# Retention then squared-ReLU FFN on one core: the second pair's v loaded before w_in, its first outputs moved ahead of the first products, and five queue places moved in the first block

## The chip, the cores and the metric

The kernel runs on one core of a Trainium2 chip. The metric is the device time of one execution in microseconds (us). Before the change it is 204.03 us, the median of three runs (203.91 to 204.12).

A core has a matrix engine (PE; its weight loads are listed as PEld), a vector engine (DVE), a scalar engine (ACT), a general engine (POOL) and a queue engine (SP) which here only issues DMA transfers. Every engine works through its own instructions in program order and waits on semaphores for the others. PE writes to PSUM; DVE and ACT read PSUM and write SBUF. POOL issues DMA transfers too.

## The reference

```python
# q, k, v: (4, 8, 768, 64); gamma[h] = 1 - 2**(-5 - h); scale = 1/8
for t in range(S):
    state = gamma * state + outer(k[:, :, t], v[:, :, t])     # 64 x 64 for each head
    y[:, :, t] = scale * (q[:, :, t] @ state)
x = y.transpose(0, 2, 1, 3).reshape(3072, 512)
h = maximum(x @ w_in, 0)                                       # w_in: 512 x 2048
out = (h * h) @ w_out                                          # w_out: 2048 x 512
```

## The kernel before

The 768 time steps of a batch are cut into chunks of 128 steps, 24 chunks in all. Within a chunk the recurrence is a masked product: scores (k against q), a mask, then outputs (v against the masked scores) plus the state of the earlier chunks against q. The outputs of a chunk are written to a tile `xt`, which is the input of the FFN. The FFN goes over blocks of chunks, `BLOCKS = [4, 2, 2, ...]`: a first product with `w_in` (in four groups of 512 columns, `w_in_bf0` to `w_in_bf3`), ReLU on ACT (L855), a square on DVE (L826), and a second product with `w_out`. The second product of most pairs of chunks uses seven half-size products instead of eight, with sums of `w_out` blocks (`sum_w_out`, L334) and of `h` blocks (L1000 in the first block, L876 later) made on DVE.

**The start (L187 to L1266) is an order written out by hand.** The first four chunks are treated as two pairs: pair 0 (chunks 0, 1) and pair 2 (chunks 2, 3). For each pair the order is: scale q and k, turn them on PE, scores (`scores_pair`, L606, whose masks are DVE instructions, L623), cast v to bf16 (`cast_pair_v`, L581: L586 on POOL, or L584 on ACT), outputs (`outputs_pair`, L657, matmuls of L666), state (`state_pair`, L634, matmuls of L642, copied to `s_bd` at L653 on ACT or L655 on DVE), and `finish_pair` (L675), which adds the state's part (L682) and copies to `xt` (L694 or L696). `first_unit` (L1103, matmuls of L846) is the first product for one chunk and one group of `w_in`; with `(0,)` it makes only the half that needs columns 0 to 255 of the group. `w_in` comes from HBM in fp32 and is cast by `cast_w` (L343), one instruction for each of the four row blocks of 128 rows and each half of 256 columns; the letters G, V, S say on which engine (POOL L351, DVE L353, ACT L355) each row block is cast. `keep_awake` (L363) are matmuls on zeros while there is nothing else for PE.

All loads of the start go through SP's one queue, in the order of L187 to L196: q and k of pair 0, k of pair 2, v of pair 0, the first half of `w_in` group 0, v of pair 2 (through `between`), the second half, the two halves of group 1, groups 2 and 3.

**From the first block on, the order is a list of places.** `ffn_pieces` (L1118) yields once for each piece of FFN work on PE, and after piece n the program emits what `put(n, ...)` has filed under n. For the first block the pieces are: 5 to 16, the first products of groups 1 to 3; 17 to 32, the second products of `last_of_first` (L979), in which `plain(j)` handles chunks 0 and 1 and the seven-product scheme chunks 2 and 3. What is emitted under the same n keeps the order in which it was filed. The pieces that matter here are

- 24 after the first half of the product with `t4`, 25 after `plain(6)`, 26 after `plain(7)` and its two output copies (L1066), 27 after the second halves of two products and `u = pb + a` (L1071, on DVE by L1000), 28 and 29 after the halves of a product into `pa`, 30 after the first half of `product(pb, s3, t3)`, which writes to the PSUM that `u` reads and takes `s3` from `third_sums`.

`attend(m, scaled, places)` (L1280) files a chunk's work: `scale_kv`, `transpose_k` (PE L419, then two ACT copies to `k_bd`, L426), `scores` (L445, mask L452 on DVE), `state` and `outputs` (L513, L521; ACT copy L529). `attend2` (L1292) does the same for chunks from 8 on, in another form: `cast_k2` (L708) on POOL, a transposing DMA on SP, `scores2` and so on. `pack_constants` (L280) makes a table of decay factors for those later chunks on POOL, DVE and ACT, and `load_w_out` (L184) issues the four loads of `w_out` from POOL's queue at places 6, 8, 11 and 14.

Of the kernel before, what the change touches and what calls it, by code (L numbers as in the profile page):

```python
# [31 lines left out]
def kernel(  # L32
# [47 lines left out]
    ps_y = ctx.enter_context(tc.tile_pool(name="ps_y", bufs=1, space=bass.MemoryType.PSUM))  # L80
# [5 lines left out]
    raw_q, raw_k, raw_v = {}, {}, {}  # L86
# [22 lines left out]
    def load_pair(m, name, src, to, heads=slice(0, H)):  # L109
        b, i = chunks[m]  # L110
        if m not in to:
            t = ldpool.tile([P, 2 * H * D], FP32, name=name)
            to[m] = t.rearrange("s (h r d) -> s r h d", h=H, r=2)
        src = src[b, heads, i * C : (i + 2) * C, :].rearrange("h (s r) d -> s h r d", r=2)
        nc.sync.dma_start(to[m].rearrange("s r h d -> s h r d")[:, heads], src)
# [57 lines left out]
    def load_w_in(g, parts=1, between=None):  # L173
        t = stage_tile(NCB * FQ).rearrange("s (c f) -> s c f", c=NCB)
        n = FQ // parts
        for j in range(parts):
            if j and between:
                between()
            nc.sync.dma_start(
                t[:, :, j * n : (j + 1) * n], w_in_v[:, :, g * FQ + j * n : g * FQ + (j + 1) * n]  # L180
            )
        staged["in", g] = t
# [7 lines left out]
    load_pair(0, "kn", k, raw_k, heads_of[1])  # L190
    load_pair(2, "kn", k, raw_k)
    load_pair(0, "vn", v, raw_v)
    load_w_in(0, parts=2, between=lambda: load_pair(2, "vn", v, raw_v))
    load_w_in(1, parts=2)
    for g in range(2, NQ):
        load_w_in(g)  # L196
# [146 lines left out]
    def cast_w(kind, g, halves=(0, 1), on="VVSG"):  # L343

        src = staged[kind, g]
        dst = (w_in_bf if kind == "in" else w_out_bf)[g]
        for half in halves:
            c = slice(half * 256, (half + 1) * 256)
            for j, engine in enumerate(on):
                if engine == "G":  # L350
                    nc.gpsimd.tensor_copy(dst[:, j, c], src[:, j, c])  # L351
                elif engine == "V":
                    nc.vector.tensor_copy(dst[:, j, c], src[:, j, c])  # L353
                else:
                    nc.scalar.activation(dst[:, j, c], src[:, j, c], AF.Copy)  # L355
# [225 lines left out]
    def cast_pair_v(m, r, on_scalar=False):  # L581
        at[m]["v"] = pair_view(v_bd2s[m // 2])
        if on_scalar:
            nc.scalar.activation(at[m]["v"][:, r], raw_v[m][:, r], AF.Copy)  # L584
        else:
            nc.gpsimd.tensor_copy(at[m]["v"][:, r], raw_v[m][:, r])  # L586
# [19 lines left out]
    def scores_pair(m, group, pools, pt):  # L606
        a = at[m]
        sts = [pool.tile([P, 2, 2, C], FP32, name=name) for pool, name in pools]
        pt = pt.rearrange("s (hh r p t) -> s hh r p t", hh=2, r=2, p=2)
        a["pt", group] = pt  # L610
        for r in range(2):
            for p in range(2):
                for hh, head in enumerate(halves):
                    for j, rows in enumerate(halves):
                        nc.tensor.matmul(
                            sts[hh][rows, r, p, :],
                            lhsT=a["kT"][head, r, 2 * group + p, j * (C // 2) : (j + 1) * (C // 2)],
                            rhs=tokens_of(m, group, p, j)[head],
                            start=True,
                            stop=True,  # L620
                        )
        def mask(hh):
            nc.vector.tensor_tensor(  # L623
                out=pt[:, hh],
                in0=sts[hh][:],
                in1=maskp.rearrange("s r q t -> s r (q t)")[:, :, None, :].to_broadcast(
                    [P, 2, 2, C]
                ),
                op=ALU.mult,
            )  # L630

        return mask
# [485 lines left out]
    def ffn_pieces(tb):  # L1118
        nch = BLOCKS[tb]
        TB = nch * C  # L1120
        if tb == 0:
            first_sums, last_sums, second_products = last_of_first()
            put(11, first_sums, 0)
            put(17, first_sums, 1)
            put(26, last_sums[0])
            put(27, last_sums[1])
            for f in range(FPQ, NFB):
                hp = ps_f.tile([P, TB], FP32, name="psf")
                first_product(tb, hp[:], f, slice(0, TB))
                relu(h_of(tb, f)[:, 0], hp)  # L1130
                yield
            yield from second_products()
            return
        elif tb <= 2:

            for c in range(nch):
                for g in range(NQ):
                    first_unit(tb, g, c)
                    if c * NQ + g in (1, 2, 3) and kept:
                        next(kept[0])  # L1140
                    if c * NQ + g == 4:
                        kept.clear()
                    if tb in SEVEN and (c, g) == (1, 3):
                        first_sums, rest = seven_products(tb)
                        first_sums(slice(0, 4))
                    yield
            if tb in SEVEN:
                yield from rest()
                return
        else:  # L1150
            h_tiles(tb)
            per = 512 // TB
            if tb in SEVEN:
                first_sums, rest = seven_products(tb)
            for f0 in range(0, NFB, per):
                hp = ps_f.tile([P, per, TB], FP32, name="psf")
                for f in range(f0, f0 + per):
                    first_product(tb, hp[:, f - f0, :], f, slice(0, TB))
                relu(h_of(tb, f0, f0 + per), hp, tb in SEVEN and f0 // per in (1, 3))
                if f0 // per in (1, 2, 3) and kept:  # L1160
                    next(kept[0])
                if f0 // per == 4:
                    kept.clear()
                if f0 // per == 5 and tb in SEVEN:
                    first_sums(slice(0, 4))
                yield
            if tb in SEVEN:
                yield from rest()
                return


        def second(op, j, g, cols=slice(0, DM)):
            for fq in range(FPQ):
                f = g * FPQ + fq
                nc.tensor.matmul(  # L1175
                    op[:],
                    lhsT=h_of(tb, f)[:, 0, j * C : (j + 1) * C],
                    rhs=w_out_bf[g][:, fq, cols],
                    start=(f == 0),
                    stop=(f == NFB - 1),  # L1180
                )

        def store(op, j, cols=slice(0, DM)):
            osb = opool.tile([P, DM], FP32, name="osb")
            nc.scalar.activation(osb[:, cols], op[:], AF.Copy)
            r0 = (first[tb] + j) * C
            nc.sync.dma_start(out[r0 : r0 + C, cols], osb[:, cols])


        for j in range(nch):  # L1190
            op = ps_f.tile([P, DM], FP32, name="psf")
            for g in range(NQ):
                second(op, j, g)
                if g == NQ - 1:
                    store(op, j)
                yield


    tp, st, f = (ps_tp, "tp"), (ps_st, "st"), (ps_f, "psf")
# [30 lines left out]
    transpose_pair_k(2, 1, *f)  # L1230
    cast_pair_v(0, 0)
    cast_pair_v(0, 1)
    mask_a = scores_pair(2, 0, (st, f), spare[:, 0:1024])
    keep_awake(2)
    end_awake()
# [4 lines left out]
    outputs_pair(0, 1)  # L1240
    mask_b = scores_pair(2, 1, (tp, f), spare[:, 1024:2048])
    mask_b(0)
    mask_b(1)
    finish_pair(0, 0)
    finish_pair(0, 1)
    state_pair(0, 1, "SV")
    cast_w("in", 0, (0,), "GGGG")
    cast_pair_v(2, 0)
    cast_pair_v(2, 1, on_scalar=True)
    first_unit(0, 0, 0, (0,))  # L1250
    first_unit(0, 0, 1, (0,))
    cast_w("in", 0, (1,), "GGVV")
    outputs_pair(2, 0, ((ps_y, "y"), st))
    outputs_pair(2, 1)
    finish_pair(2, 0)
    state_pair(2, 0, "VV")
# [15 lines left out]
    parts = {}  # L1272

    def put(place, what, *args):
        parts.setdefault(place, []).append((what, args))
# [38 lines left out]
    put(20, sum_w_out, 0)  # L1314
    put(22, sum_w_out, 1, (0, 1), slice(0, 2))
    put(24, sum_w_out, 1, (0, 1), slice(2, 4))
    put(26, sum_w_out, 1, (2, 3))
    attend(4, 12, (17, 19, 21, 23, 28))
    attend(5, None, (25, 28, 30, 32, 34))
    attend(6, 30, (33, 35, 37, 39, 42))  # L1320
    attend(7, None, (38, 42, 44, 46, 49))
    packed = pack_constants()
    put(27, next, packed)
    put(34, next, packed)
    for j, t in enumerate([s_bds[2]] + ks_bd2s + v_bd2s):
        for hh in range(2):
            put(35 + 2 * j + hh, zero_off_diagonal, t, hh)
# [1 line left out]
    for j, t in enumerate(k_big):  # L1329
# [5 lines left out]
    done = [57, 62] + [70 + 8 * j for j in range(14)]  # L1335

    ahead = {
        8: (37, 41, 44, 46, 48), 9: (0, 0, 49, 51, 53), 10: (50, 54, 55, 57, 60), 11: (0, 0, 60, 63, 68)
    }
    for m, d in zip(range(PACK_FROM, NCHUNK), done):  # L1340
        attend2(m, d, done[m - PACK_FROM - 1] if m > PACK_FROM else 0,
# [58 lines left out]
```

## Time and profile before

| | |
|---|---|
| median of three runs | 204.03 us (203.91 to 204.12) |
| profiled execution, its own time | 203.7 us |
| span of its instructions | 201.9 us |
| PE busy | 196.4 us (97%), 2403 matmuls |
| DVE busy | 148.5 us (74%) |
| ACT busy | 127.8 us (63%) |
| POOL busy | 81.1 us (40%) |
| granted PE clock | 1.0 over the whole span |

The profile is one execution. The page lists busy times, the chain of work that ended last, and groups of instructions by source line; the trace can be asked for a timeline of each engine in a stretch of time. In a timeline row the first number is the start in us from the span's start, the second the busy time, then the engine, the line, the operation, output<-input, the shapes, the number of instructions merged in the row, and in brackets the idle time before it with what ended it. Rows of 16 or 32 matmuls are one stream: the time from one matmul's start to the next is what counts, since they overlap. Some matmul records are missing from the trace (2403 of 2409).

### The profile page before, as it was taken

The numbers are of one execution on the slowest core, as the hardware profiler recorded it, in microseconds if no ns is written. First come the engines' busy times: TensorE is split into PE (matmuls) and PEld (weight loads), VectorE is DVE, ScalarE is ACT, GpSimd is POOL, SyncE is SP. The second block draws the span as 40 slices with busy tenths as digits, with TensorE's granted clock in tenths as the row PEclk, the third lists the DMA queues.
The fourth block names the chain that finished last, engine by engine and source line by source line (L and its number), as shares of the span: only waits on it lengthen the run. The fifth ranks groups of instructions, "written<-read, shape, count | busy, mean of one in ns | idle before, by whom it ended". The sixth has DMA issues, their size and how long they took to land.

```text
span 201.9 us, 5925 instructions
## 1 busy us (share of the span) xinstructions
PE 196.4 (97%) x2403; PEld 167.2 (83%) x2408; DVE 148.5 (74%) x315; ACT 127.8 (63%) x259; POOL 81.1 (40%) x152
## 2 busy tenths in 40 slices
PE   8999999999999999999999999999999999999993
PEld 8688445669965998999999999999899999999883
DVE  3987899789684678777787777777787687485374
ACT  8775875164852766783785785783775766863730
POOL 8675721099930973362622084224382022200000
PEclk9999999999999999999999999999999999999999
DMA  5999999999799999889999789999999572200202
GB/s 171 356 371 398 337 200 196 252 246 291 201 229 234 103 137 160 153 202 201 211 183 221 134 145 167 230 178 204 178 148 167 157 107 54 109 0 3 104 3 106
DMA packets 92252, 36.57 MB, mean 181 GB/s; under 512 B 68544, under 2 KB 88256, under 8 KB 92224
## 3 DMA queue, kind: packets, MB, share of 16 engines
q1 hardware_dynamic: 77312, 32.52, 68.7%
q0 software_dynamic: 14912, 3.67, 20.6%
q8 instruction: 19, 0.31, 0.6%
q14 instruction: 9, 0.07, 0.1%
HBM read 27.26 MB, written 6.29 MB: 166 GB/s over the span
## 4 chain that ended last, share of the span: by engine, by line
PE 94%; DVE 2%; ACT 1%; issue 1%; DVEq 0%
PE psf L846 42%; PE psf L880 18%; PE tp L880 7%; PE psf L1175 3%; PE psf L1039 3%; PE y L363 3%; PE psf L1004 3%; PE st L747 2%; PE y L803 2%; PE y L796 2%; PE c_ps L774 2%; PE c_ps L642 1%; PE st L445 1%; PE y L521 1%; DVE osb L876 1%
## 5 line engine op out<-in xcount | busy, mean ns | idle before, releaser
L846 PE MATMUL psf<-xt,w_in_bf 128*128 128x256 bf16 (+2 forms) x879 | 92.3, 259 | 0.1
L846 PEld LDWEIGHTS <-w_in_bf 128*128 128x128 bf16 x880 | 71.2, 98 | 11.2
L855 ACT ACTIVATE h<-psf 128x512 bf16<-128x512 f32 x96 | 56.2, 595 | 21.2 <-PE psf L846 18.9
L725 POOL COPY v_bd<-v 64x512 bf16<-64x512 bf16 x32 | 21.5, 673 | 73.7 <-DVE v L717 64.8
L826 DVE TENSOR_TENSOR h<-h 128x512 bf16<-128x512 bf16 x80 | 33.6, 433 | 21.1 <-ACT h L855 20.5
L880 PEld LDWEIGHTS <-h 128*128 128x128 bf16 x288 | 26.5, 98 | 3.0 <-DVE h L826 0.3
L160 POOL DMA_DIRECT2D k_big<-in_k_dram x32 | 21.0, 674 | 0.0
L880 PE MATMUL psf<-w_sum,h 128*128 128x256 bf16 x136 | 19.1, 273 | 0.0
L880 PE MATMUL tp<-w_out_bf,h 128*128 128x256 bf16 x136 | 19.1, 273 | 0.0
L880 PE MATMUL psf<-w_sum,k_bd 128*128 128x256 bf16 x144 | 17.9, 273 | 0.0
L876 DVE TENSOR_TENSOR u<-psf,u 128x256 f32<-128x256 f32 x18 | 7.6, 424 | 11.3 <-PE psf L880 10.9
L880 PEld LDWEIGHTS <-k_bd 128*128 128x128 bf16 x144 | 13.8, 98 | 1.5
L783 ACT ACTIVATE s_bd<-c_ps 64x256 bf16<-64x256 f32 x29 | 10.7, 370 | 6.5 <-PE c_ps L774 6.5
L876 DVE TENSOR_TENSOR osb<-psf,u 128x256 f32<-128x256 f32 x26 | 10.3, 422 | 6.1 <-PE psf L880 5.8
L376 DVE TENSOR_TENSOR qs<-qn,qf 128x512 bf16<-128x512 f32 x20 | 14.0, 704 | 0.4 <-DMA qn<-in_q_dram 0.4
L784 ACT ACTIVATE s_bd<-c_ps 64x256 bf16<-64x256 f32 x29 | 11.0, 379 | 0.4
L754 DVE TENSOR_TENSOR pt<-st,cmask 128x512 bf16<-128x512 f32 x16 | 11.0, 688 | 0.1
L717 DVE TENSOR_TENSOR v<-stage,kf 128x512 bf16<-128x512 f32 x16 | 11.0, 684 | 0.0
L916 ACT ACTIVATE osb<-tp 128x256 f32<-128x256 f32 x8 | 3.1, 385 | 12.2 <-PE tp L880 12.2
L810 ACT ACTIVATE xt<-y 128x512 bf16<-128x512 f32 x16 | 9.6, 598 | 1.8 <-PE y L803 1.2
L824 ACT ACTIVATE h<-h 128x512 bf16<-128x512 bf16 x16 | 10.1, 630 | 0.5
L876 DVE TENSOR_TENSOR k_bd<-h 128x512 bf16<-128x512 bf16 x18 | 10.1, 559 | 0.3
(151 smaller groups left out, 304.7 us busy)
## 6 DMA issues: line engine op xcount, KB each, us to landing
qn<-in_q_dram SPq DMA_DIRECT2D x12, 512.0 KB, 5.5
out_dram<-osb SPq DMA_DIRECT2D x23, 256.0 KB, 2.8
stage<-in_v_dram SPq DMA_DIRECT2D x32, 96.0 KB, 4.5
stage<-in_moe_w_in_dram SPq DMA_DIRECT2D x4, 512.0 KB, 7.6
stage<-in_moe_w_in_dram SPq DMA_DIRECT2D x2, 1024.0 KB, 8.1
w_out_bf<-in_moe_w_out_dram POOLq DMA_DIRECT2D x4, 512.0 KB, 10.2
kn<-in_k_dram SPq DMA_DIRECT2D x6, 256.0 KB, 6.0
k_big<-in_k_dram POOLq DMA_DIRECT2D x32, 48.0 KB, 4.3
```

Source lines behind the costliest of these rows:

```text
L160: nc.gpsimd.dma_start(t[rows, :, p, hh, :], k[b, 2 * p + hh, (i + 3 * n) * C : (i + 3 * n + 3) * C].rearrange("(w s) d -> s w d", s=64),)
L376: engine.tensor_tensor(out=out, in0=by, in1=table[:, :, None].to_broadcast([P, H, D]), op=ALU.mult)
L717: nc.vector.tensor_tensor(out=v2.rearrange("s (u p) d -> s u p d", u=2), in0=vn, in1=kf2[:, i, :, :, None].to_broadcast([P, 2, NPAIR, D]), ...
L725: nc.gpsimd.tensor_copy(v_bd[rows, :, hh, :], v2[rows])
L754: nc.vector.tensor_tensor(out=pt[:], in0=st[:], in1=cmask2.rearrange("s r t -> s (r t)")[:, None, :].to_broadcast([P, 2 * NPAIR, C // 2]), ...
L783: nc.scalar.activation(s_bd[halves[0], :, 0, :], c[halves[0]], AF.Copy)
L784: nc.scalar.activation(s_bd[halves[1], :, 1, :], c[halves[1]], AF.Copy)
L826: nc.vector.tensor_mul(hv, hv, hv)
L846: nc.tensor.matmul(hp, lhsT=w_in_bf[g][:, cb, fq * 128 : (fq + 1) * 128], rhs=xts[tb][:, cb, cols], start=(cb == 0), stop=(cb == NCB - 1),)
L855: nc.scalar.activation(hv, hp[:], AF.Relu)
L876: nc.vector.tensor_tensor(out=out, in0=in0, in1=in1, op=op)
L880: nc.tensor.matmul(to, lhsT=left[:, j], rhs=right(j) if callable(right) else right[:, j], start=(start and j == 0), stop=(stop and j == NF ...
```

## The change

The loads: v of pair 2 is now issued directly after v of pair 0, ahead of both halves of `w_in` group 0. The start: v of pair 2 is cast right after v of pair 0, both halves on POOL (one was on ACT); the first half of `w_in` group 0 is cast by POOL, POOL, POOL, DVE (it was POOL four times), filed between the two masks of the last scores; `outputs_pair(2, 0)` stands ahead of the two half first products instead of behind them. The places: the outputs of chunk 4 go from 28 to 24; `transpose_k` of chunk 5 from 28 to 27; `sum_w_out(1, (2, 3))` is split over 26 and 27; the third sums go from 26 to 27 and the fourth from 27 to 28; `pack_constants` goes from 27 and 34 to 12 and 15; `cast_k2` of chunk 9 goes from 49 to 47.

```diff
@@ -190,7 +190,8 @@
     load_pair(0, "vn", v, raw_v)
-    load_w_in(0, parts=2, between=lambda: load_pair(2, "vn", v, raw_v))
+    load_pair(2, "vn", v, raw_v)
+    load_w_in(0, parts=2)
     load_w_in(1, parts=2)
@@ -1122,8 +1123,8 @@
             put(11, first_sums, 0)
             put(17, first_sums, 1)
-            put(26, last_sums[0])
-            put(27, last_sums[1])
+            put(27, last_sums[0])
+            put(28, last_sums[1])
@@ -1230,6 +1231,8 @@
     cast_pair_v(0, 0)
     cast_pair_v(0, 1)
+    cast_pair_v(2, 0)
+    cast_pair_v(2, 1)
     mask_a = scores_pair(2, 0, (st, f), spare[:, 0:1024])
@@ -1240,17 +1243,15 @@
     outputs_pair(0, 1)
     mask_b = scores_pair(2, 1, (tp, f), spare[:, 1024:2048])
     mask_b(0)
+    cast_w("in", 0, (0,), "GGGV")
     mask_b(1)
     finish_pair(0, 0)
     finish_pair(0, 1)
     state_pair(0, 1, "SV")
-    cast_w("in", 0, (0,), "GGGG")
-    cast_pair_v(2, 0)
-    cast_pair_v(2, 1, on_scalar=True)
+    outputs_pair(2, 0, ((ps_y, "y"), st))
     first_unit(0, 0, 0, (0,))
     first_unit(0, 0, 1, (0,))
     cast_w("in", 0, (1,), "GGVV")
-    outputs_pair(2, 0, ((ps_y, "y"), st))
     outputs_pair(2, 1)
     finish_pair(2, 0)
     state_pair(2, 0, "VV")
@@ -1314,14 +1315,15 @@
-    put(26, sum_w_out, 1, (2, 3))
-    attend(4, 12, (17, 19, 21, 23, 28))
-    attend(5, None, (25, 28, 30, 32, 34))
+    put(26, sum_w_out, 1, (2,))
+    put(27, sum_w_out, 1, (3,))
+    attend(4, 12, (17, 19, 21, 23, 24))
+    attend(5, None, (25, 27, 30, 32, 34))
     attend(6, 30, (33, 35, 37, 39, 42))
     attend(7, None, (38, 42, 44, 46, 49))
     packed = pack_constants()
-    put(27, next, packed)
-    put(34, next, packed)
+    put(12, next, packed)
+    put(15, next, packed)
@@ -1335,7 +1337,7 @@
     ahead = {
-        8: (37, 41, 44, 46, 48), 9: (0, 0, 49, 51, 53), 10: (50, 54, 55, 57, 60), 11: (0, 0, 60, 63, 68)
+        8: (37, 41, 44, 46, 48), 9: (0, 0, 47, 51, 53), 10: (50, 54, 55, 57, 60), 11: (0, 0, 60, 63, 68)
     }
```

## The prediction

> **What bounds the kernel now.** I read the chain of waits first, then the timelines of PE, DVE, ACT and POOL up to 60 us, then the waits of PE. The chain is PE's nearly from end to end, so what the change is worth is what it does to gaps on PE.
>
> ```profile
> PE 94%; DVE 2%; ACT 1%; issue 1%; DVEq 0%
> ```
>
> The same engine's timeline, at the start and in the middle of the first block:
>
> ```profile
> 14.26 1.07 PE L846 MATMUL psf<-xt,w_in_bf 128*128 128x128 bf16 x16
> ...
> 15.30 0.24 PE L666 MATMUL y<-h,v_bd 64*64 64x128 bf16 x1
> ...
> 16.24 0.62 PE L642 MATMUL c_ps<-v_bd,ks_bdp 64*128 64x128 bf16 x8
> 16.79 1.14 PE L846 MATMUL psf<-xt,w_in_bf 128*128 128x128 bf16 x16
> ...
> 44.34 0.60 PE L1004 MATMUL psf<-w_sum,h 128*128 128x256 bf16 x4 [0.21 <-DVE u L1000]
> ...
> 45.25 0.34 PE L445 MATMUL st<-qT,k_bd 128*128 128x128 bf16 x3 [0.26 <-ACT k_bd L426]
> ```
>
> In a row of n matmuls with 128 columns the starts lie 0.056 us apart ((1.07 - 0.23)/15), with 256 columns 0.109 ((0.60 - 0.27)/3). Where the matmul's tile shape changes, the next start comes 0.15 after the last one: 0.09 lost. Counting so from start to start, PE's real waits between 13 and 60 us are small: 0.05 before 15.30 (v's cast), 0.07 after 16.79 (a cast of w_in), 0.37 at 44.34, 0.42 at 45.25, 0.07 at 46.37, 0.19 at 58.89 (chunk 6's mask). Nothing else is to be had. What the start waits for is read on POOL:
>
> ```profile
> 10.56 1.16 POOL L586 CAST v_bd<-vn 128x512 bf16<-128x512 f32 x2
> 11.89 1.43 POOL L351 CAST w_in_bf<-stage 128x256 bf16<-128x256 f32 x4 [0.17 <-DMA stage<-in_moe_w_in_dram]
> 14.64 0.61 POOL L586 CAST v_bd<-vn 128x512 bf16<-128x512 f32 x1 [1.31 <-DMA vn<-in_v_dram]
> 15.93 0.92 POOL L351 CAST w_in_bf<-stage 128x256 bf16<-128x256 f32 x2 [0.69 <-DMA stage<-in_moe_w_in_dram]
> ...
> 55.31 1.44 POOL L708 CAST ks_bdp<-stage 64x512 bf16<-64x512 f32 x2
> ```
>
> By SP's issues and their times to landing, v of pair 0 landed at 10.50, the first half of w_in at 11.84, v of pair 2 at 14.58, the second half at 15.88. Each is 512 KB; the first, second and fourth follow the one before in 1.3 to 1.5, but v of pair 2 took 2.74. The trace has sixteen completion marks for each load: fifteen of v's came by 13.39, the last at 14.58. What stands beside it is one 16 KB instruction packet, started at 11.92 and busy for 0.95:
>
> ```profile
> q8 instruction: 1, 0.02, 4.0%
> ```
>
> That queue brings nineteen such packets, one for each 120 to 380 (mostly some 270) of PE's instructions; this one comes at PE's 309th, at the state of pair 0 (11.90). One of the sixteen shares is held up behind it, and every later load of the start has its sixteenth mark about 1.2 late as well.
>
> **The start.** PE's program is the same up to 12.9, so the packet comes at 11.92 again, and the same loads lie ahead of that point in the queue, in another order: v of pair 2 lands at about 12.0 (10.50 + 1.5), or 12.97 if its last share is caught; the first half of w_in then takes the place of v at 14.58. The bounds are 13.4 (its fifteen unharmed shares) and 14.6; I take 14.58, since the bytes up to there are the same.
>
> POOL casts v of pair 2 by 13.2 to 14.2. PE has finished pair 0's second state at 14.11 (last start) and does `outputs_pair(2, 0)` from 14.26 (16 matmuls, 0.23). Then the first products wait for casts. POOL's casts of w_in start 0.05 after landing and 0.34 apart ((1.43 - 0.40)/3), so the three end at 15.03, 15.38 and 15.72; the third releases PE's third matmul at 15.76, and 13 more starts (0.72) bring the last one to 16.48. `outputs_pair(2, 1)` 16.63, `finish_pair(2, 0)` 16.99, the state 17.31 where it was 16.24: 1.07 late. The first products after it (16.79 before) lost 0.07 to a cast that will then be done. Net **+1.0**, with bounds of 0.05 (w_in at 13.4: casts done at 14.5, and one more change of tile shape, 0.09, against 0.05 of wait saved) and 1.1. Even on time the second half of w_in, cast by 16.86, holds PE where it was: nothing is gained at the start.
>
> On DVE the one cast of w_in now waits for 14.58 with the second mask, the s_bd copy of L655, two casts and two more copies behind it. The mask (0.68) ends at 15.6 and the copy at 16.0; PE wants them at 16.63 and 16.99: hidden behind POOL's casts. Without that cover (w_in at 13.4) the mask is on time anyway. ACT loses one cast (0.63) and POOL gains 0.61 in a wait of 1.31; neither is on the path. On SP nothing but the order of two issues changes.
>
> **pack_constants** moves 2.1 us of POOL work (40.95 to 43.22) between w_out's third and fourth load, issued at 24.97 and 25.70. The four land 7.0 to 13.5 after issue, 3.4 apart behind one another, so the fourth is queued, not late: 0. If it did land 2.1 later, at 41.3, DVE's sums at 40.10 (41.1 with the start's delay) would lose 0.2. Its 0.7 on DVE and 0.24 on ACT go to place 15; DVE has 0.66 idle before 36.76.
>
> **The middle, times as before.** DVE now stands so:
>
> ```profile
> 41.80 0.68 DVE L341 TENSOR_TENSOR w_sum<-w_out_bf 128x1024 bf16<-128x1024 bf16 x1
> 42.40 0.72 DVE L341 TENSOR_TENSOR w_sum<-w_out_bf,w_sum 128x1024 bf16<-128x1024 bf16 x1
> 43.04 0.79 DVE L1000 TENSOR_TENSOR h<-h 128x512 bf16<-128x512 bf16 x2
> 43.86 0.42 DVE L1000 TENSOR_TENSOR u<-psf,u 128x256 f32<-128x256 f32 x1
> ```
>
> After the change chunk 4's outputs (12 matmuls, 0.67) come at 39.38, and `pb`'s last matmul starts at 42.75; `u` can start at 43.07 instead of 43.86. Behind it are the second w_sum (0.6) and the third sums, which `product(pb, s3, t3)` needs as much as `u`: 43.07 + 0.34 + 0.60 + 0.41 = 44.42, so PE is released at 44.46, where it was 44.34. The wait stays; the third sums are late now. Chunk 5's k is turned at 42.86, ACT is free of its two output copies at 43.55, and the two k_bd copies end at 44.7 before the scores at 44.90: that 0.42 goes. Chunk 5's second scores wait for the first's mask, behind the fourth sums on DVE: 46.12 against 45.99. First product of the next block at 46.34 instead of 46.59: **-0.25**. Bounds: -0.87 (all three waits gone) and +0.1 (the third sums cost as much as the k copies give).
>
> **Chunk 9's cast.** POOL made it at 67.27; it now follows chunk 8's at 56.7, for another 1.44. Under chunk 8's cast a DVE square took 0.83 and a scaling 1.10, where 0.41 and 0.68 are usual:
>
> ```profile
> 55.45 0.83 DVE L826 TENSOR_TENSOR h<-h 128x512 bf16<-128x512 bf16 x1
> 56.20 1.10 DVE L376 TENSOR_TENSOR ks<-kn,kf 128x512 bf16<-128x512 f32 x1
> 57.22 0.68 DVE L376 TENSOR_TENSOR qs<-qn,qf 128x512 bf16<-128x512 f32 x1
> ```
>
> So the scaling at 57.22 stretches by 0.42 (the square behind it starts after the cast), chunk 6's mask at 58.16 slips by as much, and PE already waits for it at 58.89. **+0.4**, bounds -0.19 (no stretch, and the wait goes) and +0.8 (both stretched). Nothing behind it waits now for chunk 9's k, whose DMA transpose has slack, so no gain.
>
> **Sum.** 203.7 + 1.0 - 0.25 + 0.4 = 204.85 for the profiled execution (span 201.9 and 1.8 around it); the median lies 0.33 above that execution: **205.2**.
>
> The Trainium skill's page "Runtime: NRT & Kernel Launch", section "Instruction fetch mechanics", says that crossing a 16 KiB block of instructions costs "one DMA tail-bump, mostly hidden". By it the load beside the packet would not be late, w_in would land at 13.4 and the sum would be 204.2. The trace agrees for PE itself, which runs on, but not for the load.
>
> **The rivals.**
> - *On time* (14%): the packet's delay falls on a share that has slack, w_in lands near 13.4. For it: fifteen of sixteen marks. Against: every load after 11.92 had a late mark. 204.03 + 0.05 - 0.25 + 0.4 = 204.2, within noise.
> - *DVE's queue drains, faster* (13%): with `u` ahead of a w_sum and the third sums, and the decay table off its queue, DVE is no longer late for PE anywhere between 41 and 59, and the waits at 44.34, 45.25, 46.37 and 58.89 (0.87 + 0.19) all go. With w_in on time: 204.03 + 0.05 - 1.06 = 203.0. It decides as long as the start costs less than 1.06; at the forecast's start it just cancels it, 204.0. For it: `u` waits behind 1.4 of sums now. Against: the third sums are wanted at the same point of PE as `u`, and now stand behind it.
> - *POOL's double cast* (8%): both DVE instructions are stretched, with the forecast's start. 204.03 + 1.0 - 0.25 + 0.8 = 205.6.
>
> **How the numbers follow.** The forecast has 65%. Its own range runs from 204.6 (the middle or the cast at its better bound) to 206.0 (all three at their worse ones). The whole range goes down to 203.7 to take in the on-time case with some of the middle; it leaves out the faster case and a little above 205.9. This measurement tells about 0.2% (0.4 us) from no change. Faster: 0.13, and 0.01 of the on-time case. Same: the other 0.13 of that, and 0.02 of the forecast. Slower: the remaining 0.63 and 0.08.
>
> **What would show it.** Right: POOL's w_in casts start near 14.6 with the wait on the w_in load, PE's first L846 has gaps of 0.3 there and the L846 row of 16.79 stands near 17.8; the L1004 row after `u` still waits, on third sums; L445 does not wait for k_bd; two POOL casts in a row near 56, and a longer wait of L521 on chunk 6's mask. Wrong: w_in's casts at 13.4, or no instruction packet near 11.9; then the sum drops by 1.0.

## The result, and the profile after

The changed kernel takes 205.59 us (median of six runs, 205.03 to 205.62), the kernel before beside it 204.06 us (six runs, 203.91 to 204.57): a ratio of 1.0067, 95% interval 1.0052 to 1.0082. It is slower by 1.5 us. The profiled execution took 205.59 us itself, and its span grew from 201.9 to 203.8 us. Lines from L194 on are numbered one higher in it, at the very end two.

The span can be cut at three points of PE that both traces have: the start of the first product with 512 columns (the start is over), the first product of the second block, and the first product of the third block. The table gives the first of them and the two stretches between them, in us, for all kernels that are spoken of below; from the third point to the last matmul it is 133.24 in each of them but one (133.73 in "the same, packet late"). Two of the 28 executions of the four kernels whose `w_in` lands late ("after", "new start alone", "after, chunk 9's cast back", "after, all casts on POOL") ran some 3 us longer at a mean granted clock of 0.98: one of 207.68 us, which is the traced one of "after, chunk 9's cast back" (hence its 24.81), and one of 208.52 us, which widens the interval of "after, all casts on POOL".

| kernel | median, us (runs) | ratio to before, 95% | start ends | first block | second block |
|---|---|---|---|---|---|
| before | 204.03 | | 20.53 | 26.07 | 18.71 |
| after | 205.59 (6) | 1.0067 (1.0052 to 1.0082) | 21.89 | 25.86 | 19.45 |
| after, old start | 204.23 (11) | 1.0011 (1.0003 to 1.002) | 20.67 | 25.86 | 19.35 |
| new start alone | 204.86 (6) | 1.0041 (1.0027 to 1.0054) | 21.74 | 26.07 | 18.62 |
| after, chunk 9's cast back | 204.77 (12) | 1.0037 (1.0029 to 1.0046) | 24.81 | 25.86 | 18.62 |
| after, packet late | 204.67 (9) | 1.004 (1.0024 to 1.0056) | 20.80 | 25.86 | 19.35 |
| after, all casts on POOL | 205.73 (4) | 1.0133 (1.006 to 1.0205) | 21.98 | 25.87 | 19.44 |
| middle alone | 203.96 (12) | 1.0008 (0.9996 to 1.0021) | 20.56 | 25.87 | 18.94 |
| middle, third sums first | 203.14 (12) | 0.997 (0.9958 to 0.9983) | 20.68 | 25.51 | 18.62 |
| the same, packet late | 203.88 (12) | 0.999 (0.9975 to 1.0005) | 20.96 | 25.51 | 18.62 |
| the same, new start, packet late | 203.45 (12) | 0.9989 (0.9976 to 1.0002) | 20.80 | 25.51 | 18.62 |

So the change cost 1.36 at the start, gave back 0.21 in the first block, and cost 0.74 in the second: 1.89, the whole growth of the span.

**The start.** The chain of waits, by engine, as the page of the changed kernel has it:

```profile
PE 84%; DVE 5%; DMA 4%; SPq 3%; issue 1%; ACT 1%; POOL 1%; DVEq 0%
```

PE had 94% of it before. The same chain of the changed kernel in order of time (start, length, what) shows what took PE's place at the start:

```profile
7.50 7.22 DMA stage<-in_moe_w_in_dram
14.77 1.23 POOL w_in_bf L352 x3
16.04 0.96 PE psf L847 x14
```

The first half of `w_in` was issued at 7.50 and landed 7.2 later; three casts of it and then PE follow one another without slack. POOL's timeline of the changed kernel:

```profile
12.09 1.18 POOL L587 CAST v_bd<-vn 128x512 bf16<-128x512 f32 x2 [0.35 <-DMA vn<-in_v_dram]
14.77 2.09 POOL L352 CAST w_in_bf<-stage 128x256 bf16<-128x256 f32 x5 [1.50 <-DMA stage<-in_moe_w_in_dram]
...
54.20 2.19 POOL L374 MEMSET v_bd<- 64x512 bf16 x4
56.45 3.40 POOL L709 CAST ks_bdp<-stage 64x512 bf16<-64x512 f32 x4
```

The v of pair 2 is early now (cast from 12.09, before from 14.64), and POOL idles 1.50 for `w_in` instead of 1.31 for v. The completion marks of the load say why: fifteen of its sixteen shares landed between 13.10 and 13.41, the last at 14.71. The 16 KB instruction packet started at 11.59 and took 0.93. In the timeline of PE the delay goes straight through:

```profile
15.35 1.65 PE L847 MATMUL psf<-xt,w_in_bf 128*128 128x128 bf16 x16 [0.66 <-POOL w_in_bf L352]
...
17.60 0.62 PE L643 MATMUL c_ps<-v_bd,ks_bdp 64*128 64x128 bf16 x8
18.15 1.07 PE L847 MATMUL psf<-xt,w_in_bf 128*128 128x128 bf16 x16
...
44.45 1.04 PE L1005 MATMUL psf<-w_out_bf,h 128*128 128x256 bf16 x8
45.92 0.61 PE L1005 MATMUL psf<-w_sum,h 128*128 128x256 bf16 x4 [0.43 <-DVE h L1001]
46.36 0.39 PE L446 MATMUL st<-qT,k_bd 128*128 128x128 bf16 x4
...
59.63 0.39 PE L522 MATMUL y<-pt,v_bd 128*128 128x128 bf16 x4
60.78 0.38 PE L522 MATMUL y<-pt,v_bd 128*128 128x128 bf16 x4 [0.76 <-DVE pt L453]
```

Sixteen matmuls with 128 columns take 1.65 (1.07 before) and begin 1.09 later; the state stands at 17.60 instead of 16.24, and the next products at 18.15 instead of 16.79.

**The first and second block.** In the same rows, PE no longer waits for `k_bd` at 46.36. It does wait at 45.92, and the releaser is `h` of L1001, the third sums, no longer `u`. At 60.78 it waits for chunk 6's mask: from start to start 0.92 are lost there. In the kernel before, the same eight matmuls lost 0.19 and stand in one row of PE's timeline:

```profile
58.48 0.79 PE L521 MATMUL y<-pt,v_bd 128*128 128x128 bf16 x8
```

DVE's timeline of the changed kernel has both causes:

```profile
44.50 0.42 DVE L1001 TENSOR_TENSOR u<-psf,u 128x256 f32<-128x256 f32 x1 [0.95 <-ACT osb L1067]
44.84 0.68 DVE L342 TENSOR_TENSOR w_sum<-w_out_bf,w_sum 128x1024 bf16<-128x1024 bf16 x1
45.44 0.75 DVE L1001 TENSOR_TENSOR h<-h 128x512 bf16<-128x512 bf16 x2
...
56.50 0.83 DVE L827 TENSOR_TENSOR h<-h 128x512 bf16<-128x512 bf16 x1
57.26 1.10 DVE L377 TENSOR_TENSOR ks<-kn,kf 128x512 bf16<-128x512 f32 x1
58.28 1.09 DVE L377 TENSOR_TENSOR qs<-qn,qf 128x512 bf16<-128x512 f32 x1
59.30 0.83 DVE L827 TENSOR_TENSOR h<-h 128x512 bf16<-128x512 bf16 x1
60.05 0.68 DVE L453 TENSOR_TENSOR pt<-st,cmask 128x512 bf16<-128x512 f32 x1
```

`u` is done in time, then one sum of `w_out` blocks and then the sums that PE needs next. Later, four operations in a row run beside POOL's four casts (56.45 to 59.85), and all four are stretched, not two.

### The profile page after: what moved, and what is told of

It reads as the page before. It is cut to its first block, busy times and chain, and to the rows that moved or that the text cites. A ratio compares the mean times of both kernels' runs of the same rounds, so it can differ in the third digit from the quotient of the medians.

```text
span 203.8 us, 5932 instructions
## 1 busy us (share of the span) xinstructions
PE 196.3 (96%) x2408; PEld 166.6 (82%) x2408; DVE 148.1 (73%) x316; ACT 127.4 (63%) x258; POOL 81.6 (40%) x152
## 4 chain that ended last, share of the span: by engine, by line
PE 84%; DVE 5%; DMA 4%; SPq 3%; issue 1%; ACT 1%; POOL 1%; DVEq 0%
PE psf L847 39%; PE psf L881 18%; PE tp L881 7%; DMA stage<-in_moe_w_in_dram 4%; PE psf L1040 3%; SPq L115 3%; PE psf L1005 3%; PE psf L1176 3%; PE st L748 2%; PE y L804 2%; PE y L797 2%; PE c_ps L775 2%; DVE h L827 1%; PE y L522 1%; PE st L446 1%
## 5 line engine op out<-in xcount | busy, mean ns | idle before, releaser
L827 DVE TENSOR_TENSOR h<-h 128x512 bf16<-128x512 bf16 x80 | 34.1, 440 | 22.6 <-ACT h L856 22.3
```

What stands on the lines that cost most here:

```text
L827: nc.vector.tensor_mul(hv, hv, hv)
```

## The experiments

**The start taken back.** The changed kernel with the loads and the hand-written start of the kernel before.

```diff
-    load_pair(2, "vn", v, raw_v)
-    load_w_in(0, parts=2)
+    load_w_in(0, parts=2, between=lambda: load_pair(2, "vn", v, raw_v))
...
-    cast_pair_v(2, 0)
-    cast_pair_v(2, 1)
...
-    cast_w("in", 0, (0,), "GGGV")
...
-    outputs_pair(2, 0, ((ps_y, "y"), st))
+    cast_w("in", 0, (0,), "GGGG")
+    cast_pair_v(2, 0)
+    cast_pair_v(2, 1, on_scalar=True)
     first_unit(0, 0, 0, (0,))
     first_unit(0, 0, 1, (0,))
     cast_w("in", 0, (1,), "GGVV")
+    outputs_pair(2, 0, ((ps_y, "y"), st))
```

> The changed kernel with the loads and the hand-written start of the kernel before; the moved places stay. If the start costs 1.36 us (the first block's 512-column products begin at 21.89 instead of 20.53 in the trace), the time falls from 205.6 to about 204.2 to 204.6, the first products are back at 14.26 and chunk 6's mask still holds PE for some 0.9. Rival, that the places cost most of it: it stays above 205.2.

Measured: 204.23 us, 1.36 less than the whole change. `w_in` landed at 11.85 again and v of pair 2 at 14.77 with its last share. The start is the larger part of the loss, and the moved places together cost 0.2 to 0.3 us in the median. Chunk 6's mask held PE for 0.50 (at 59.47) and not for the 0.9 expected; the other part of the long second block is a wait of 0.31 for a scaling at 47.97, which the experiment with the moved places alone explains.

**The new start alone.** The reverse: the kernel before with only the new loads and start.

> The kernel before with the loads and the hand-written start of the changed one, all places as before. If the start costs 1.36, 205.4; the middle then shows the old waits of 0.37 and 0.42 and chunk 6's mask the old 0.19, unless a later start gives slack there. Rival, that the start's delay is absorbed later: 204.1.

Measured: 204.86 us, some 0.5 less than expected. The start cost 1.21 in this trace (`w_in` landed at 14.57), 0.15 less than in the changed kernel. In the second block the wait for chunk 6's mask fell from 0.19 to 0.09 (18.62 instead of 18.71), while the waits of the first block stayed. The other 0.3 lies in the starting value: the profiled execution of the kernel before is 0.33 below its median, that of this kernel on its median. The timeline of PE in this kernel:

```profile
45.85 0.23 PE L446 MATMUL st<-qT,k_bd 128*128 128x128 bf16 x1
46.47 0.34 PE L446 MATMUL st<-qT,k_bd 128*128 128x128 bf16 x3 [0.39 <-ACT k_bd L427]
...
59.69 0.70 PE L522 MATMUL y<-pt,v_bd 128*128 128x128 bf16 x8
```

The `k_bd` wait that the moved places take away is here; the eight matmuls of L522 run in one row.

**Chunk 9's cast back at 49.** The changed kernel with one number changed.

```diff
-        8: (37, 41, 44, 46, 48), 9: (0, 0, 47, 51, 53), ...
+        8: (37, 41, 44, 46, 48), 9: (0, 0, 49, 51, 53), ...
```

> The changed kernel with chunk 9's cast at its old place alone. If POOL's two casts in a row cost PE the 0.74 by which the wait on chunk 6's mask grew, 204.85, with DVE's 1.09 scaling and 0.83 square behind the ks scaling back at 0.68 and 0.41 and the wait near 0.19. Rival, that the mask is late because DVE starts that stretch late: 205.6.

Measured: 204.77 us, 0.82 less than the whole change; the second block is 0.83 shorter. Its trace is of the execution of 207.68 us, which lost 2.9 us before 24 us, as the last section shows. From there on its rows can be read. DVE's timeline in this kernel, some 2.9 us later than in the changed kernel:

```profile
59.43 0.83 DVE L827 TENSOR_TENSOR h<-h 128x512 bf16<-128x512 bf16 x1
60.19 1.09 DVE L377 TENSOR_TENSOR ks<-kn,kf 128x512 bf16<-128x512 f32 x1
61.20 0.68 DVE L377 TENSOR_TENSOR qs<-qn,qf 128x512 bf16<-128x512 f32 x1
61.81 0.41 DVE L827 TENSOR_TENSOR h<-h 128x512 bf16<-128x512 bf16 x1
62.14 0.68 DVE L453 TENSOR_TENSOR pt<-st,cmask 128x512 bf16<-128x512 f32 x1
```

Without the second pair of casts the second scaling takes 0.68 instead of 1.09 and the square behind it 0.41 instead of 0.83: 0.41 and 0.42, together the 0.83 that PE waited longer in the changed kernel. The wait for the mask that is left is 0.09, where some 0.19 was expected.

**The instruction packet moved.** The changed kernel with the zero matmuls of `keep_awake` four times as wide and a quarter as many, so that PE has 108 instructions fewer ahead of the same work and fetches its next 16 KB later.

```diff
-    nc.vector.memset(still, 0.0)
+    wide = spare[:, 4096 - 4 * P : 4096]
+    nc.vector.memset(wide, 0.0)
...
-        for _ in range(4 * n):
-            nc.tensor.matmul(idle_ps[0][:], lhsT=still, rhs=still, start=True, stop=True)
+        for _ in range(n):
+            nc.tensor.matmul(idle_ps[0][:], lhsT=still, rhs=wide, start=True, stop=True)
```

> The changed kernel with every four 128-column warm-up matmuls on zeros replaced by one of 512 columns: the same PE time, 108 fewer PE instructions ahead of the first products, nothing else. If the load of w_in is late because of the instruction packet at PE's 309th instruction, the packet now comes about 13.1 to 13.4, the load lands near 13.4 to 13.9 and the time falls by about 1.0 to 1.3, to 204.3 to 204.6. Rival, that the load is late because of its place behind two v loads of 512-byte rows: it lands at 14.7 again and the time stays at 205.6.

Measured: 204.67 us, 0.1 above the range expected. The packet came at 14.55, later than the 13.1 to 13.4 expected, and the sixteen shares of `w_in` between 13.06 and 13.38, with no straggler. Place in the queue, bytes and neighbours were the same, so it is the packet that delayed the last share. The delay moved along with it: of the first half of `w_in` group 1 fifteen shares landed by 16.10 and the last at 17.38. POOL's timeline in this kernel:

```profile
12.04 1.17 POOL L588 CAST v_bd<-vn 128x512 bf16<-128x512 f32 x2 [0.32 <-DMA vn<-in_v_dram]
13.43 1.15 POOL L353 CAST w_in_bf<-stage 128x256 bf16<-128x256 f32 x3 [0.22 <-DMA stage<-in_moe_w_in_dram]
```

The timeline of PE: the first products run without a gap.

```profile
14.59 1.07 PE L848 MATMUL psf<-xt,w_in_bf 128*128 128x128 bf16 x16
```

The start ends at 20.80, 1.09 sooner than in the changed kernel, and 0.27 later than in the kernel before. Of that 0.25 is a gap between two matmuls of the state (16.50 to 16.80) in which the trace shows no wait.

**All four casts of `w_in`'s first half on POOL.** The changed kernel with `"GGGG"` where it has `"GGGV"`.

> The changed kernel with the one cast of w_in's first half that DVE makes given back to POOL. In the trace of the changed kernel POOL's first cast there took 0.52 and began together with DVE's; the others took 0.40. If DVE's cast holds POOL's up, the first cast is 0.40 again and PE's first product starts 0.1 sooner after the landing, but the fourth row block comes 0.34 after the third, so the first block's 512-column products start within 0.1 of 21.89 and the time is 205.5 to 205.7. Rival, that POOL's first cast after a wait is slow in any case: 0.52 again, and the time 0.2 higher.

Measured: 205.73 us in the median, where 205.5 to 205.7 was expected. POOL's timeline in this kernel:

```profile
14.70 2.23 POOL L352 CAST w_in_bf<-stage 128x256 bf16<-128x256 f32 x6 [1.50 <-DMA stage<-in_moe_w_in_dram]
```

Without DVE's cast beside it, POOL's first cast takes 0.40 and releases PE at 15.15; in the changed kernel it takes 0.52 and PE comes at 15.35. POOL's fourth cast then costs more than that: PE's fourth matmul waits until 16.18, and the start ends at 21.98, 0.09 later.

**The moved places alone, chunk 9's cast at its old place.** The kernel before with the places 12 to 28 of the change.

> The kernel before with the moved places of the first block alone: old loads, old hand-written start, chunk 9's cast at its old place. In the traces so far the stretch from the first 512-column product to the next block's first product is 25.86 us with the moved places and 26.07 without, whatever the start; so 0.2 below the kernel before, 203.75. Rival, that the places pay only with a late start: 204.0.

Measured: 203.96 us, no gain: the number is the rival's. The first block is 0.20 shorter, as expected, and the second 0.23 longer. DVE's timeline of this kernel:

```profile
46.07 1.73 DVE L376 TENSOR_TENSOR qs<-qn,qf 128x512 bf16<-128x512 f32 x2
```

Two scalings of 0.68 take 1.28 together in the kernel before (46.24). Here the second runs from 46.67 to 47.80, 1.13 long, and PE waits 0.31 for it at 47.85, inside this row:

```profile
47.32 0.93 PE L406 MATMUL tp<-ident,qs 128*128 128x128 bf16 x8
```

Beside it is POOL's timeline:

```profile
46.64 0.61 POOL L392 CAST v_bd<-vn 128x512 bf16<-128x512 f32 x1
```

In the kernel before, this cast of v came at 48.94, since `pack_constants` stood ahead of it on POOL:

```profile
48.94 0.61 POOL L392 CAST v_bd<-vn 128x512 bf16<-128x512 f32 x1
```

With that moved to places 12 and 15 the cast falls on DVE's scaling. In the changed kernel it misses it by 0.05: the cast ends at 47.35 and the scalings start at 47.40, because the start is a microsecond late. Where the moved places stand behind an early start ("after, old start" and "after, packet late"), the second scaling begins 0.02 after the cast and takes 1.13 again.

**The third sums ahead of the last sum of `w_out` blocks.** The kernel just shown, with the sums that PE does not need yet filed later.

```diff
-            put(28, last_sums[1])
+            put(31, last_sums[1])
...
-    put(27, sum_w_out, 1, (3,))
+    put(28, sum_w_out, 1, (3,))
```

> The same, with the third sums directly behind u on DVE, the second half of the last w_sum behind them (place 28) and the fourth sums at place 31. If the third sums, queued behind that w_sum, are what PE's 0.59 wait after u is for, the wait falls to at most 0.1 and the stretch of 25.86 to 25.3 to 25.5: 203.2 to 203.5. Rival, that the wait only moves to the next thing DVE makes (the mask of chunk 5's first scores, or q of chunk 6): 203.75.

Measured: 203.14 us, ratio 0.997 (0.9958 to 0.9983): faster than both kernels. DVE's timeline of this kernel:

```profile
43.30 0.43 DVE L1000 TENSOR_TENSOR u<-psf,u 128x256 f32<-128x256 f32 x1 [0.66 <-ACT osb L1066]
43.64 0.75 DVE L1000 TENSOR_TENSOR h<-h 128x512 bf16<-128x512 bf16 x2
44.31 0.69 DVE L341 TENSOR_TENSOR w_sum<-w_out_bf,w_sum 128x1024 bf16<-128x1024 bf16 x1
```

And PE's:

```profile
43.25 1.04 PE L1004 MATMUL psf<-w_out_bf,h 128*128 128x256 bf16 x8
44.13 0.60 PE L1004 MATMUL psf<-w_sum,h 128*128 128x256 bf16 x4
44.56 0.63 PE L445 MATMUL st<-qT,k_bd 128*128 128x128 bf16 x4
```

The wait after `u` (0.59 in the changed kernel) is gone. Of it 0.23 comes back at once as a wait for `k_bd` inside the row at 44.56, which the other wait had covered; the first block ends 0.36 sooner. DVE's second scaling now starts at 46.44, ahead of POOL's cast at 46.77, and keeps its 0.68.

**The packet late, in that kernel.** The same with the wide zero matmuls, still with the old start.

> The previous kernel with the 512-column warm-up matmuls, which put the packet 108 instructions later. If the packet is also what made v of pair 2 late in the old order, v lands at 13.4 and the second half of w_in at 14.7, and the waits of 0.05 on v's cast and 0.07 on w_in's cast go: 0.1 less than the previous one at best, the same within noise at worst. Rival, that the old order made v late: it still lands at 14.6.

Measured: 203.88 us, in the median 0.74 above the previous kernel, where 0 to 0.1 less was expected; the two intervals overlap a little. v of pair 2 did land at 13.40 instead of some 14.6 to 14.8: in the old order it was this load that the packet delayed. But the time did not follow: there is again a gap without a wait in the state's matmuls (0.45, 16.46 to 16.97), and in the profiled execution PE lost 0.49 up to 69.93 to a wait for a transpose on SP's queue. The gap in PE's timeline:

```profile
16.23 0.45 PE L643 MATMUL c_ps<-v_bd,ks_bdp 64*128 64x128 bf16 x5
16.97 0.32 PE L643 MATMUL c_ps<-v_bd,ks_bdp 64*128 64x128 bf16 x3 [0.29 <-issue]
```

**Everything at its best place.** The same again with the change's loads and start.

> The same with the changed kernel's loads and start. With w_in on time the new start has one more change of tile shape (0.09) and no wait on v's cast, so 0 to 0.1 above the previous kernel. Rival, that the new start is worth something once w_in is on time: 0.2 or more below it.

Measured: 203.45 us, ratio 0.9989 (0.9976 to 1.0002). `w_in` landed at 13.42 and the start ended at 20.80 (a gap of 0.22 again at 16.5), against 20.68 with the old start and the packet where it was. The median is 0.43 below that of the previous kernel, which is the rival's number, but the ratios to the kernel before are 0.9989 and 0.999, with nearly the same interval. In the traces the two kernels differ by the 0.49 of the transpose and by their gaps; without the gaps (0.22 and 0.45) the new start ends 0.07 later than the old one. So with its load on time no worth of the new start is shown, and no loss that can be measured.

## Why the prediction was right, and where its sizes were off

- **Direction and cause of the start.** Right. `w_in` took the place of v beside the packet, its last share was late by 1.3, and nothing was gained from the earlier v. Moving the packet alone took away 1.09 of the 1.36, and 0.25 of what was left is the gap in the state. The rival "on time" describes the kernel with the packet late, not this one. The rule quoted from the Trainium skill's page "Runtime: NRT & Kernel Launch", section "Instruction fetch mechanics", that crossing a 16 KiB block is "mostly hidden", held for PE in the changed kernel, which shows no gap beside the packet, and not for the load: 1.09 of the start went with the packet. (The packets of the kernel before follow one another after 119 to 320 of PE's recorded instructions, where the prediction has 120 to 380; nothing rests on this.)
- **Size of the start.** The term "+1.0" was 1.36. The landing was 14.71 and not 14.58 (0.13; the other kernels with this order and the early packet have 14.57 to 14.75). "Three casts 0.34 apart" held for two of three: the first took 0.52, because DVE's cast of the fourth row block ran beside it, so the third ended at 15.98 instead of 15.72. The state came at 17.60, 0.29 later than worked out. The saving of 0.07 on a later cast was there, and as much was lost at 19.00 on DVE's copy of `s_bd`. The bound of 1.1 was too low: it had the landing at 14.6 at the latest, held DVE's cast for hidden because it was off the path, and left out what it does to POOL.
- **The middle.** "-0.25" was -0.21, by the mechanism that was named: `u` early, the third sums late (0.59 at 45.92 where some 0.5 was worked out) and the `k_bd` wait gone. For the mask of chunk 5's first scores a wait of 0.13 was worked out; it was 0.07, as before. The rival "DVE's queue drains" fell on this point; with the two sums exchanged, 0.65 of its 1.06 came true (0.56 in the first block, 0.09 in the second).
- **pack_constants.** "0" was right for `w_out`: its fourth load was issued at 27.82 instead of 25.70 and landed at 39.37 instead of 39.19. What the step did not see was POOL's own queue: a cast of v moves forward by 2.3 us. In the changed kernel it costs nothing by 0.05 us; in the kernel with the moved places alone it cost the 0.31 that ate the gain.
- **Chunk 9's cast.** "+0.4" was +0.74, near the upper bound. Here the forecast's mechanism failed and that of the rival "POOL's double cast" held: both DVE instructions were stretched. The casts were taken to end just before the square. But beside DVE's work POOL's casts slow down too (0.61, 0.70, 0.95 and 0.98): the four took 3.40, where twice 1.44 was counted, and so reached the square at 59.30.
- **The sum.** The spans differ by 1.89, where 1.15 was worked out. The median moved by only 1.53, because the profiled execution of the kernel before (203.7) lay 0.3 below its median, that of the changed kernel on its median. The prediction added 0.33 for this on both sides; so the total came out only 0.4 short. That it missed by 0.4 and not by the 0.74 of the spans is luck. So is the exact number of the rival "POOL's double cast", 205.6: it had the cast right and the start at 1.0.

What stays open is the gap of 0.22 to 0.45 without a wait in the three kernels with wide zero matmuls. The traces point to PE waiting for its instructions, though no run tests it: in all three the gap stands behind PE's 448th recorded instruction and ends 2.21 to 2.28 after the packet started (14.55, 14.68 and 14.58). In the eight kernels with the early packet the 449th instruction starts 2.25 to 2.80 after the packet, and there is no gap. It was not tried to put chunk 9's cast on another engine.

## What to carry to other kernels

A load is there when its last share is there; where one share is held up by something else on the same DMA engine, the question is which load stands there, and it should be one with slack. When an instruction is moved forward on an in-order engine, look at what PE needs next behind it: here `u` was early for nothing until the third sums came directly after it. And work that leaves POOL's queue pulls POOL's casts forward, onto whatever DVE then does.

## What the runs showed of the hardware

**Of DVE and POOL, the one that starts later was stretched.** DVE's scaling beside POOL's cast of v took 1.13 when it began 0.03 after the cast, and the cast its usual 0.61. Where the scaling began 0.33 before the cast, it took 0.68 and the cast 0.83. At the start the same is seen between casts: POOL's took 0.52 instead of 0.40 when DVE's began 0.03 before it. Where several stand in a row, each begins while one of the other engine runs, and both are stretched: in the changed kernel the scalings took 1.10 and 1.09 and POOL's last two casts 0.95 and 0.98. Masks, which read PSUM, kept 0.68 to 0.69 beside POOL's casts (in the changed kernel 0.69 from 46.79, the cast beside it 0.62 from 46.73).

**The clock can fall without a long idle time.** In the trace of the kernel with chunk 9's cast back, the busy times by stretch were (stretch, length, then busy time and instructions of PE, PEld, DVE, ACT and POOL, then the granted clock, the DMA share and GB/s):

```profile
10.00:14.00 4.00, 3.93 (x117) 3.07 (x115) 3.45 (x6) 2.61 (x7) 2.90 (x5) 1.00 1.11 367
14.00:16.00 2.00, 1.14 (x24) 0.60 (x21) 1.24 (x4) 0.75 (x2) 1.20 (x3) 1.00 1.09 385
16.00:17.00 1.00, 0.93 (x13) 0.93 (x14) 0.97 (x3) 0.00 (x0) 0.82 (x3) 0.76 1.09 387
17.00:18.00 1.00, 1.00 (x22) 0.63 (x21) 0.04 (x1) 0.00 (x0) 0.56 (x2) 0.50 1.12 427
...
23.00:24.00 1.00, 1.00 (x17) 1.00 (x16) 1.00 (x4) 0.55 (x1) 0.94 (x3) 0.83 1.18 327
```

PE's longest wait here was 0.86 us, and yet the clock stood at 0.50 from 16.5 to 23.3, which cost some 3 us. What triggered it was not isolated: in the trace of the changed kernel PE is busy for the same 1.14 us from 14 to 16 and waits 0.82, and the clock stays at 1.00. The Trainium skill's page "TensorE: Matmul & The Clock Gate", section "Part 1: The HAM clock gate", has the clock fall after an idle window of about 3.4 us; this row shows it falling after 2 us in which PE was busy for 57%.

**The instruction fetch is not free for others.** With the early packet PE itself ran on, but one packet of 16 KB, busy for 0.92 to 0.95 us, made one share of each of the next loads 1.1 to 1.4 us later than the other fifteen.
